# Scores of two batches joined into operations over eight array tiles, in a kernel of landmark attention, routed experts and a second layer

## The chip, the cores and the metric

One core of a Trainium2 chip runs the whole kernel. The metric is device microseconds of one execution, as the median of three runs; less is better. TensorE (PE in the profile) does the matrix products, VectorE (DVE), ScalarE (ACT) and GpSimd (POOL) the rest, and the queue of SyncE (SP) starts most of the loads.

## The reference

Three stages follow one another (4 batches, 8 heads, 576 tokens, head width 64).

```python
q_lm = q.reshape(B, H, 32, S // 32, D).mean(axis=3)      # 32 landmarks, k_lm alike
A, Bm, C = sm(q, k_lm), sm(q_lm, k_lm), sm(q_lm, k)      # sm: softmax of scaled products
Z = 2 * Z - Z @ Bm @ Z                                   # six times
x = A @ Z @ C @ v                                        # 2304 tokens x 512
h = np.maximum(x[mask] @ w1[e], 0.0)                     # e: the expert of a token, of 8
y[mask] = gate_w[mask, None] * (h @ w2[e])
r = np.maximum(y @ w_in, 0.0)                            # 512 -> 2048
out = (s * (r * r) + b) @ w_out                          # 2048 -> 512
```

`A` needs the scores of all queries with the 32 key landmarks, `C` those of the 32 query landmarks with all keys. `w_in` and `w_out` arrive as float64.

## The kernel before, in words

**A planner orders everything.** The kernel is written as a list of operations (`A(...)`, which is `Plan.add`): each has an engine or a choice of engines, a guessed duration, the buffers that it reads and writes, and a priority. `Plan.run` takes, again and again, the operation that can start first (ties by priority, then by order of writing), gives it its place in the 798 units of SBUF (256 bytes of each partition) or in the 8 banks of PSUM, and advances that engine's clock. The order of each engine that results is written into the program. So an engine works its list in order: if the chip is later at one operation than the plan had it, all behind it on that engine wait too. Where an operation may go to two engines, the planner takes the one with the earliest end, with a handicap from `TUNE["bias"]` (0.7 us against DVE, nothing against ACT or POOL): `copy` chooses between ACT and DVE, `two` and `minus` between DVE and POOL. `caps` in `Plan(...)` (L350) limits how many buffers of a name live at once.

**Attention, per batch (`attention`, L525 on).** Sums over 18 tokens make the landmarks (L558 to L565, in tile `ss`). The scores are matmuls of 64 rows by 32 columns, 288 tokens wide: `cs` (L656 to L665) for `C` and `as` (L715 to L725) for `A`. The eight heads of a batch are held as two groups `g` of four. One operation does one group: eight matmul calls, which are 16 matmul records in the trace, on four tiles of the array (two halves of the rows, each paired with two of the four strips of 32 columns), into two banks. So a batch has two `cs` and two `as` operations, each free to start when its own group is ready. After `cs` come the maximum on DVE (L671), the exponential on ACT (L679) and transposes (L687); after `as` a transpose on DVE (L730) and the softmax, whose subtraction and product are `two` operations. `TOOK` holds measured durations by name (0.75 for `cs` and `as`), and they replace the guess in the call.

**Experts.** The kernel reads which expert a batch's first token goes to, loads that expert's weights (`w1s`, `w2s`), folds the value side into the first weight (`v1`, L945) and does both layers (`experts`; all large products go through `mm3`, L972, which multiplies a high and a low part: three matmuls for one). The operation `v1` is 16 matmul records of 64 rows by 32 columns, 256 wide, on all eight tiles of the array, into two banks. The expert work of one batch runs on TensorE between the attention steps of the next ones.

**Conversion of the float64 weights (`convert`, L1037 on).** 32 loads of 512 KB (L1039) go into buffers `sg`, of which five may live at once; each takes six steps on DVE, ACT and POOL (the last is L1054) to become half of a tile `w32i` or `w32o`.

**Second layer (`layer2`, L1163 on).** Three groups G of 768 tokens, each with eight units j. A unit is seven products of 2 x 2 blocks (`prod`, each six matmuls of 384 columns), the sums of which are combined (L1198), squared on ACT and DVE (L1202, L1203), split in a high and a low part (`gh` L1206 on ACT, `rr` L1208 on DVE), and eight products with `w_out` (sums in L1250). Group 0 also prepares the parts of the weights (`weights`, `outer`, by `copy` and `minus`, L508 and L1076) and stores them; groups 1 and 2 load them back. `tokens` prepares the seven right operands of a group: loads, four sums (`tq`, L1076), then for each operand a high part `th` (a `copy`) and a low part (a `minus`). It is called for the next group in unit 7, with two gates: the first (`early`, the first product of unit 6) for the loads, the sums and the high parts of two operands, and the second (`mark`, the fifth of the seven products of unit 7) for the high parts of the five others.

Of the kernel before, what the change touches and what calls it, by code (L numbers as in the profile page):

```python
# [18 lines left out]
B, H, S, D = 4, 8, 576, 64  # L19
N, DM, E, F, DFF = B * S, H * D, 8, 1024, 2048  # L20
LM, SEG = 32, 18
NB = 288
# [296 lines left out]
TUNE = {"ahead": (6,), "t_at": lambda st: [st[B - 1]["l1half"]], "w_at": lambda st: [st[B - 1]["l1first"]], "blk": "AADD", "pre": 2, "bias": {"DVE": 0.7, "ACT": 0.0},  # L319
# [20 lines left out]
def moe_kernel(ctx, tc, qT, kT, va, vb, emb, tau, w1, w2, win, wout, s_in, b_in, outT):  # L340
    nc = tc.nc
# [8 lines left out]
    plan = Plan({"S": NS, "PS": 8}, {"sg": 5, "acc": 2, "hp": 3, "vp": 1, "w2h": 6, "w2s": 8, "v1h": 3, "v1l": 3, "w1s": 4,  # L350
# [174 lines left out]
    def attention(b, gate):  # L525
# [62 lines left out]
        def f():  # L588
            for p in range(4):
                for h in range(2):  # L590
                    nc.tensor.matmul(bs.t[row(p, h), p // 2, 0:32], ql(p)[half_(h)], kl(p)[half_(h)],
                                     start=True, stop=True)
# [65 lines left out]
        for g in range(2):  # L658
            def f(g=g):
                for hf in range(2):  # L660
                    for x in range(2):
                        for h in range(2):
                            nc.tensor.matmul(cs[g].t[row(2 * g + x, h), hf, 0:NB], ql(2 * g + x)[half_(h)],  # L663
                                             k[g][x].t[half_(h), NB * hf:NB * hf + NB], start=True, stop=True)
            A("PE", 1.07, f, r=[QS[2 * g], QS[2 * g + 1], *k[g]], w=[cs[g]], prio=pr + 3, kind="cs")  # L665
# [48 lines left out]
        am = small("am", 2, [128, 2, 2, 18])  # L714
        for g in range(2):  # L715
            aps = P("aps")
            at, tt = ats[g], S_([128, S], nm="tt")

            def f(g=g, aps=aps):
                for hf in range(2):  # L720
                    for x in range(2):
                        for h in range(2):
                            nc.tensor.matmul(aps.t[row(2 * g + x, h), hf, 0:NB], kl(2 * g + x)[half_(h)],  # L723
                                             q[g][x].t[half_(h), NB * hf:NB * hf + NB], start=True, stop=True)
            z["as"] = A("PE", 1.07, f, r=[KS[2 * g], KS[2 * g + 1], *q[g]], w=[aps], prio=pr + 4, kind="as")  # L725
# [437 lines left out]
    def layer2(G):  # L1163
# [7 lines left out]
        def unit(j, last, early):  # L1171
# [59 lines left out]
            if G + 1 < NG and j == 7:  # L1231
                tokens(G + 1, [early], [mark])
# [158 lines left out]
```

## Time and profile before

| | us |
|---|---|
| median of 3 runs (688.82 to 690.6) | 689.05 |
| the profiled execution, its own time | 693.66 |
| its span, first to last instruction | 691.8 |
| TensorE busy in the span | 648.0 |
| VectorE busy | 470.5 |
| ScalarE busy | 314.3 |
| GpSimd busy | 249.8 |

The profiled execution is 4.6 us longer than the median, and 1.9 us of its time lie outside of its span. A busy time is the union of an engine's instructions; a matmul's end is modelled, so starts are the surer measure of how closely matmuls follow one another. A row of busy time by stage gives the window and its length, then busy us and number of instructions of TensorE's matmuls, its weight loads, VectorE, ScalarE and GpSimd, then TensorE's granted clock as a share of 2.4 GHz, the busy share of the DMA engines and GB/s. In a list of waits a row says which instruction sat idle until which other one ended: in all, how often, and the longest.

### The profile page before, as it was taken

Reading aid. Unit: us, or ns where it says so; the run is one execution under the profiler, and the core shown is the slowest. Engines: PE = TensorE matmul, PEld = TensorE weight load, DVE = VectorE, ACT = ScalarE, POOL = GpSimd, SP = SyncE. Lnnn points to the kernel's source line nnn. Section 1 sums busy time; section 2 is a strip of 40 time slices with the busy share of each in tenths; the row PEclk is TensorE's granted clock in tenths of the full one; section 3 lists DMA queues with packets and bytes.
Section 4 is the critical chain, followed back from the end, with each engine's and each line's share of the span. In section 5 each row is a group of like instructions: output and inputs, shape, how many; then the busy total and the mean of one; then the engine's idle time right before and its main releaser. Section 6 shows DMA issues by size and latency. Waiting matters only on the chain.

```text
span 691.8 us, 13145 instructions
## 1 busy us (share of the span) xinstructions
PE 648.0 (94%) x5070; PEld 599.4 (87%) x5070; DVE 470.5 (68%) x971; ACT 314.3 (45%) x662; POOL 249.8 (36%) x213
## 2 busy tenths in 40 slices
PE   8789899999889998989989989999999999999995
PEld 5557778878779998978888989999999899999995
DVE  6775686688679667889899788635546744465552
ACT  2256426726445644565454464534333544333431
POOL 3641535634444574695755775000003600000000
PEclk9899999999999999999999999999999999999999
DMA  6617586575364655254747557875448476564202
GB/s 217 227 41 262 188 254 229 189 268 174 117 213 139 237 181 184 100 228 180 260 176 238 197 212 247 287 242 206 145 167 285 154 267 236 186 197 168 92 0 97
DMA packets 55577, 132.99 MB, mean 192 GB/s; under 512 B 5024, under 2 KB 25032, under 8 KB 55504
## 3 DMA queue, kind: packets, MB, share of 16 engines
q1 hardware_dynamic: 46208, 101.74, 43.7%
q10 hardware_dynamic: 9296, 30.30, 11.2%
q8 instruction: 42, 0.69, 0.4%
q14 instruction: 31, 0.25, 0.1%
HBM read 98.19 MB, written 33.84 MB: 191 GB/s over the span
## 4 chain that ended last, share of the span: by engine, by line
PE 70%; DVE 16%; ACT 5%; issue 3%; DMA 3%; POOL 1%; SPq 0%; ACTq 0%; DVEq 0%; POOLq 0%
PE big L972 60%; DVE rr L1203 3%; DVE rr L1208 2%; DMA w1s<-in_w 2%; PE big L723 1%; PE big L436 1%; PE big L825 1%; PE big L663 1%; PE big L644 1%; DVE sums L1250 1%; ACT rr L1202 1%; PE big L945 1%; DVE tq L1076 1%; DVE sg L1042 1%; DVE xx L1198 1%
## 5 line engine op out<-in xcount | busy, mean ns | idle before, releaser
L972 PE MATMUL big<-gh,rp 128*128 128x384 f32 x256 | 85.9, 335 | 1.1 <-DVE sums L1250 1.1
L972 PE MATMUL big<-rr,rp 128*128 128x384 f32 x256 | 85.6, 335 | 0.4 <-DVE rr L1208 0.4
L972 PE MATMUL big<-gh,rq 128*128 128x384 f32 x256 | 85.5, 334 | 0.0
L972 PE MATMUL big<-hh,w2h 128*128 128x288 f32 x256 | 79.1, 309 | 0.6 <-DVE hl L1000 0.6
L1208 DVE SCALAR_TENSOR_TENSOR rr<-rr,bbc,gh 128x384 fp32r<-128x384 f32 x96 | 68.9, 732 | 14.7 <-ACT gh L1206 14.7
L1250 DVE TENSOR_TENSOR sums<-big,sums 128x384 f32<-128x384 f32 x84 | 46.5, 553 | 46.9 <-PE big L972 46.4
L1206 ACT ACTIVATE gh<-rr,bbc 128x384 fp32r<-128x384 f32 x96 | 58.5, 616 | 43.3 <-DVE rr L1203 42.7
L972 PE MATMUL big<-hl,w2h 128*128 128x288 f32 x256 | 75.8, 296 | 0.0
L972 PE MATMUL big<-hh,w2s 128*128 128x288 f32 x256 | 75.5, 295 | 0.0
L972 PE MATMUL big<-th,rh 128*128 128x384 f32 x224 | 75.0, 335 | 0.0
L1203 DVE SCALAR_TENSOR_TENSOR rr<-xx,sbc,rr 128x384 f32<-128x384 f32 x72 | 64.2, 894 | 15.8 <-ACT rr L1202 14.6
L1198 DVE TENSOR_TENSOR xx<-big,xx 128x384 f32<-128x384 f32 x72 | 39.8, 554 | 50.4 <-PE big L972 48.2
L508 ACT COPY xx<-big 128x384 f32<-128x384 f32 x71 | 33.4, 470 | 80.5 <-PE big L972 80.2
L1202 ACT ACTIVATE rr<-xx 128x384 f32<-128x384 f32 x72 | 37.6, 523 | 43.4 <-DVE xx L1198 43.4
L972 PEld LDWEIGHTS big<-hh,w2h 128*128 128x128 f32 x256 | 48.2, 188 | 4.9 <-issue 3.1
L972 PEld LDWEIGHTS big<-gh,rp 128*128 128x128 f32 x256 | 48.0, 188 | 1.9 <-DVE sums L1250 1.7
L972 PEld LDWEIGHTS big<-rr,rp 128*128 128x128 f32 x256 | 48.1, 188 | 0.8 <-DVE rr L1208 0.8
L972 PE MATMUL big<-gh,oh 128*128 128x384 f32 x128 | 44.0, 344 | 5.0 <-DVE sums L1250 3.9
L972 PE MATMUL big<-ah,v1h 128*128 128x288 f32 x128 | 42.0, 328 | 7.0 <-DVE hl L1000 3.5
L972 PEld LDWEIGHTS big<-hh,w2s 128*128 128x128 f32 x256 | 48.4, 189 | 0.0
L972 PEld LDWEIGHTS big<-hl,w2h 128*128 128x128 f32 x256 | 48.4, 189 | 0.0
L972 PEld LDWEIGHTS big<-gh,rq 128*128 128x128 f32 x256 | 48.1, 188 | 0.0
(235 smaller groups left out, 1727.2 us busy)
## 6 DMA issues: line engine op xcount, KB each, us to landing
rh<-sw_d SPq DMA_DIRECT2D x16, 896.0 KB, 7.0
w1s<-in_w SPq DMA_DIRECT2D x16, 512.0 KB, 6.6
w2s<-in_w SPq DMA_DIRECT2D x16, 512.0 KB, 5.3
sg<-in_win SPq DMA_DIRECT2D x16, 512.0 KB, 4.4
sg<-in_wout SPq DMA_DIRECT2D x16, 512.0 KB, 4.5
rx<-sw_d SPq DMA_DIRECT2D x16, 512.0 KB, 4.1
rp<-so_d SPq DMA_DIRECT2D x16, 512.0 KB, 4.0
rq<-so_d SPq DMA_DIRECT2D x16, 512.0 KB, 4.5
```

Source lines behind the costliest of these rows:

```text
L436: nc.tensor.matmul(warm.t[:, 0:128], zero.t, zero.t, start=True, stop=True)
L508: nc.scalar.copy(out=out(), in_=in_()) if e == "ACT" else nc.vector.tensor_copy(out=out(), in_=in_())
L644: nc.tensor.matmul(xp.t[r_, 64 * g + 32 * lo:64 * g + 64], cur()[r_, g, 0, :], cur()[r_, g, lo:2, :], start=True, stop=True)
L663: nc.tensor.matmul(cs[g].t[row(2 * g + x, h), hf, 0:NB], ql(2 * g + x)[half_(h)], k[g][x].t[half_(h), NB * hf:NB * hf + NB], start=True, s ...
L723: nc.tensor.matmul(aps.t[row(2 * g + x, h), hf, 0:NB], kl(2 * g + x)[half_(h)], q[g][x].t[half_(h), NB * hf:NB * hf + NB], start=True, sto ...
L972: nc.tensor.matmul(out, w, x, start=s, stop=e, skip_group_check=more)
L1198: A("DVE", d_dve(NT), lambda: nc.vector.tensor_tensor(out=x.t, in0=pv(k)(), in1=x.t, op=ALU.add), r=[bank[k]], w=[x], prio=pu, kind="l6")
L1202: A("ACT", d_actp(NT), lambda: nc.scalar.activation(out=rr[i].t, in_=src(), func=AF.Relu), r=[b], w=[rr[i]], prio=pu, kind="rr")
L1203: A("DVE", d_dve(NT), lambda: nc.vector.scalar_tensor_tensor(out=rr[i].t, in0=src(), scalar=sbc[:, 0:1], in1=rr[i].t, op0=ALU.mult, op1=AL ...
L1206: A("ACT", d_act(NT), lambda: nc.scalar.activation(out=gh[i].t, in_=rr[i].t, func=AF.Identity, bias=bbc[:, 0:1]), r=[rr[i], (c_sb, 1)], w= ...
L1208: A("DVE", d_dve(NT), lambda: nc.vector.scalar_tensor_tensor(out=low(rr[i]), in0=rr[i].t, scalar=bbc[:, 0:1], in1=gh[i].t.bitcast(F32), op ...
L1250: nc.vector.tensor_tensor(out=sums[dc].t, in0=ac.t[:, 0:NT], in1=sums[dc].t, op=ALU.add)
```

## The change

`cs` and `as` become one function, `scores`. For batches 2 and 3 it makes one operation of both groups, with the matmul calls of the two groups in turn; its names `cs2` and `as2` have no entry in `TOOK`, so the planner takes 1.2 us for it. For batches 0 and 1 there are still two operations. DVE's handicap goes from 0.7 to 0.3 us, the cap of `sg` from five to four, and the second gate of `tokens` becomes the first.

```diff
-TUNE = {"ahead": (6,), "t_at": ..., "bias": {"DVE": 0.7, "ACT": 0.0},
+TUNE = {"ahead": (6,), "pairs": 2, "t_at": ..., "bias": {"DVE": 0.3, "ACT": 0.0},
...
-    plan = Plan({"S": NS, "PS": 8}, {"sg": 5, "acc": 2, ...
+    plan = Plan({"S": NS, "PS": 8}, {"sg": 4, "acc": 2, ...
...
-        for g in range(2):
-            def f(g=g):
-                for hf in range(2):
-                    for x in range(2):
-                        for h in range(2):
-                            nc.tensor.matmul(cs[g].t[row(2 * g + x, h), hf, 0:NB], ql(2 * g + x)[half_(h)],
-                                             k[g][x].t[half_(h), NB * hf:NB * hf + NB], start=True, stop=True)
-            A("PE", 1.07, f, r=[QS[2 * g], QS[2 * g + 1], *k[g]], w=[cs[g]], prio=pr + 3, kind="cs")
+        def scores(lm, keys, src, dst, prio, kind):
+
+            for gs in ([(0, 1)] if b >= TUNE["pairs"] else [(0,), (1,)]):
+                def f(gs=gs):
+                    for hf in range(2):
+                        for x in range(2):
+                            for h in range(2):
+                                for g in gs:
+                                    nc.tensor.matmul(dst[g].t[row(2 * g + x, h), hf, 0:NB], lm(2 * g + x)[half_(h)],
+                                                     src[g][x].t[half_(h), NB * hf:NB * hf + NB], start=True, stop=True)
+                o = A("PE", 1.2, f, r=[r for g in gs for r in (keys[2 * g], keys[2 * g + 1], *src[g])], w=[dst[g] for g in gs],
+                      prio=prio, kind=kind + "2" if len(gs) > 1 else kind)
+            return o
+        scores(ql, QS, k, cs, pr + 3, "cs")
...
+        ap2 = [P("aps") for _ in range(2)]
+        z["as"] = scores(kl, KS, q, ap2, pr + 4, "as")
...
-                tokens(G + 1, [early], [mark])
+                tokens(G + 1, [early], [early])
```

The loop over the two groups behind `as` now takes its bank pair from `ap2`; the matmuls in it are gone.

## Rows read from the trace of the kernel before

**Rows 1.** The page: span, and busy us of the engines.

```profile
span 691.8 us, 13145 instructions
...
PE 648.0 (94%) x5070; PEld 599.4 (87%) x5070; DVE 470.5 (68%) x971; ACT 314.3 (45%) x662; POOL 249.8 (36%) x213
```

**Rows 2.** Busy time by stage, columns as told under the table of times.

```profile
0.00:80.00 80.00, 65.60 (x914) 49.17 (x915) 53.87 (x174) 35.37 (x96) 37.43 (x63) 0.94 0.55 187
80.00:178.00 98.00, 97.05 (x1204) 80.28 (x1202) 72.34 (x233) 47.91 (x114) 43.91 (x37) 1.00 0.64 209
178.00:203.00 25.00, 20.24 (x180) 17.89 (x179) 18.68 (x52) 12.79 (x33) 12.08 (x7) 0.93 0.64 211
203.00:264.00 61.00, 60.67 (x476) 58.40 (x476) 45.06 (x93) 30.33 (x58) 32.35 (x23) 0.97 0.55 188
264.00:287.40 23.40, 20.77 (x145) 20.48 (x144) 18.51 (x28) 12.71 (x23) 12.09 (x8) 0.93 0.33 112
287.40:427.60 140.20, 128.17 (x697) 119.53 (x696) 121.59 (x156) 74.61 (x141) 95.26 (x70) 1.00 0.56 212
427.60:552.00 124.40, 122.81 (x703) 121.36 (x702) 73.03 (x120) 51.35 (x100) 16.68 (x8) 1.00 0.63 215
552.00:684.70 132.70, 132.66 (x765) 132.34 (x764) 66.83 (x122) 49.17 (x99) 0.00 (x0) 1.00 0.46 160
```

**Rows 3.** Waits of TensorE from 178 to 287.4 us: total, times, longest.

```profile
PE big L972 <- DVE hl L1000: 3.5, 2, 2.6
PE big L972 <- DVE rt L886: 2.8, 1, 2.8
```

**Rows 4.** Waits of TensorE in second-layer group 0, 287.4 to 427.6 us.

```profile
PE big L972 <- DVE xx L1198: 4.3, 5, 1.3
PE big L972 <- DVE sums L1250: 3.9, 5, 1.3
```

**Rows 5.** Chain that ended last, 80 to 155 us: start, length, what.

```profile
80.40 0.59 PE big L945 x16
...
91.34 1.10 PE big L723 x16
92.45 0.97 PE big L663 x16
...
96.00 1.10 PE big L723 x16
...
99.81 1.10 PE big L663 x16
...
153.72 1.10 PE big L663 x16
```

**Rows 6.** Waits of TensorE from 80 to 178 us.

```profile
PE big L972 <- DVE hl L1000: 0.6, 1, 0.6
```

**Rows 7.** The tile of the token operands: duration ns min/median/max, first and last start.

```profile
L508 ACT CAST th<-tq x9: 816/824/837, 273.6 to 545.0; 128x768 fp32r<-128x768 f32 x9
```

**Rows 8.** Waits of TensorE from 427.6 to 552 us.

```profile
PE big L972 <- DVE sums L1250: 1.1, 2, 0.7
```

**Rows 9.** VectorE by shape, group 0: count, busy us, mean ns, idle before.

```profile
L1203 DVE SCALAR_TENSOR_TENSOR rr<-xx,sbc,rr 128x384 f32<-128x384 f32 x24 | 32.4, 1361 | 6.6 <-ACT rr L1202 5.7
...
L1076 DVE TENSOR_TENSOR ol<-w32o,oh 128x512 fp32r<-128x512 f32 x1 | 1.2, 1225 | 0.0
```

**Rows 10.** VectorE by shape, group 2 (552 to 684.7 us).

```profile
L1203 DVE SCALAR_TENSOR_TENSOR rr<-xx,sbc,rr 128x384 f32<-128x384 f32 x24 | 14.7, 612 | 3.7 <-ACT rr L1202 3.6
```

**Rows 11.** GpSimd by shape, group 0.

```profile
L1076 POOL TENSOR_TENSOR ol<-w32o,oh 128x512 fp32r<-128x512 f32 x15 | 19.7, 1337 | 10.2 <-ACT oh L508 10.2
...
L1054 POOL TENSOR_TENSOR w32i<-w32i,sg 128x512 int32<-128x512 int32 x4 | 6.1, 1540 | 12.9 <-DVE w32i L1051 12.9
L1054 POOL TENSOR_TENSOR w32o<-w32o,sg 128x512 int32<-128x512 int32 x4 | 5.7, 1419 | 8.1 <-DVE w32o L1051 8.1
```

**Rows 12.** The page, loads: KB of one, us from issue to landing.

```profile
sg<-in_win SPq DMA_DIRECT2D x16, 512.0 KB, 4.4
```

More of the change, by code (lines that the diff above doesn't have):

```diff
@@ L316, in d_dma @@
     return nbytes / RATE
-TUNE = {"ahead": (6,), "t_at": lambda st: [st[B - 1]["l1half"]], "w_at": lambda st: [st[B - 1]["l1first"]], "blk": "AADD", "pre": 2, "bias": {"DVE": 0.7, "ACT": 0.0},
+TUNE = {"ahead": (6,), "pairs": 2, "t_at": lambda st: [st[B - 1]["l1half"]], "w_at": lambda st: [st[B - 1]["l1first"]], "blk": "AADD", "pre": 2, "bias": {"DVE": 0.3, "ACT": 0.0},
         "flex": {"w2l": "P", "al": "P"}, "fill": 45.0, "slack": 0.05, "duty": 0.45, "first": 12,
@@ L348, in moe_kernel @@
     dr = ctx.enter_context(tc.tile_pool(name="dr", bufs=1, space=DRAM))
-    plan = Plan({"S": NS, "PS": 8}, {"sg": 5, "acc": 2, "hp": 3, "vp": 1, "w2h": 6, "w2s": 8, "v1h": 3, "v1l": 3, "w1s": 4,
+    plan = Plan({"S": NS, "PS": 8}, {"sg": 4, "acc": 2, "hp": 3, "vp": 1, "w2h": 6, "w2s": 8, "v1h": 3, "v1l": 3, "w1s": 4,
                                      "hh": 5, "hl": 5, "acc2": 4, "accr": 1, "gh": 8, "rr": 8, "xx": 4, "hp2": 3,
@@ L714, in attention @@
         am = small("am", 2, [128, 2, 2, 18])
+        ap2 = [P("aps") for _ in range(2)]
+        z["as"] = scores(kl, KS, q, ap2, pr + 4, "as")
         for g in range(2):
[L716 to L725, printed above, removed]
+            aps, at, tt = ap2[g], ats[g], S_([128, S], nm="tt")
             th = lambda tt=tt: tt.t.rearrange("p (a b) -> p a b", b=32)
```

## The prediction

> **What bounds the kernel now.** I read the page first, for the share of each engine, then busy time by stage, then TensorE's waits in the stages where it idles, and then the chain of waits around the scores. The page shows TensorE busy for 648.0 of 691.8 us and VectorE, the next, for 470.5 [rows 1]: the kernel is a string of matmuls with 43.8 us of holes. The stages tell where the holes are, as length less TensorE's busy time [rows 2]: 14.4 us before 80, 1.0 from 80 to 178, 4.8 to 203, 0.3 to 264, 2.6 to 287.4, 12.0 in group 0 of the second layer, 1.6 in group 1, none in group 2, and 7.1 behind the last matmul. So from 80 to 178 us, where the scores of batches 2 and 3 lie, TensorE is the bound: whatever is taken off its list there, the rest moves up by. In group 0 it waits for VectorE, which is busy for 121.6 of 140.2 us.
>
> The holes after 178 us are late answers of VectorE rather than a lack of matmuls: waits for `hl` and for one copy, `rt` [rows 3], and in group 0 for `xx` and `sums` [rows 4]. An early hole costs a second time: in the windows where the granted clock stands below 1.00 (0.93 of 25 us, 0.97 of 61, 0.93 of 23.4) about 1.7 us each are lost, since TensorE runs at 1.2 in place of 2.4 GHz for a while after it has idled [rows 2].
>
> **The change, part by part. The scores.** In the chain a score operation moves TensorE on by 0.97 to 1.10 us for 16 matmul records, and there are eight for batches 2 and 3; the first four and the last are shown [rows 5]. Four `as` at 1.10 and four `cs` at 0.97, 1.10, 1.10 and 1.10 make 8.67 us, which go. In their place come four operations of 32 records. The nearest row is `v1`: also 64 rows by 32 columns, but on all eight tiles, and its 16 records take 0.59 us for 256 columns [rows 5]. With t for a turn of the tiles per column and f for what an operation costs once, `v1` is f + 2 x 256 t = 0.59 and a score operation, on four tiles, f + 4 x 288 t = 1.10; so t is 0.80 ns and f 0.18 us. Were `v1`'s eight tiles served four at a time, it would be f + 4 x 256 t, and f would come out as -3.5 us, which can't be: eight tiles do run abreast there. The joined operation has 32 records on eight tiles, four turns again: 1.10 us. Four of them are 4.40, and 4.3 us are saved. Bounds: scaling `v1` plainly gives 2 x 0.59 x 288/256 = 1.33 us each, a saving of 3.4; if the second group waits for the first, nothing is saved. I take 4.3, as `v1` has the same tiles and the same two-bank pattern.
>
> Here a page speaks against the change. The Trainium skill (TensorEngine Tiling (Array Packing), Gotcha 1: PSUM Pressure) says that tiles in different rows of the array cannot write one PSUM bank at the same time, and both row halves of each group write one bank. By that rule the joined operation would take turns and the saving would be 0; the trace disagrees, because `v1` does the same with 0.59 us.
>
> **What joining makes wait.** The joined operation needs the sums of all eight heads and four free banks of eight at once. In batch 2 the first `as` starts at 91.34 and the second at 96.00 us, and the first `cs` at 92.45 and the second at 99.81 [rows 5]; so the first group's softmax begins up to 5 to 7 us later. That is covered: expert matmuls of the batch before fill TensorE to 178 us with 1.0 us of holes [rows 2]. What isn't covered is a wait of the operation itself, since TensorE takes its list in order and every expert matmul (L972) behind it stands still. The nearest wait in this stage is 0.6 us [rows 6], the worst behind it 2.8, for a bank that a late VectorE copy gave back [rows 3]. I take one of 0.6 us; the bounds are none and 2.8 us for each of four. Sum for the scores: -4.3 + 0.6 = -3.7.
>
> **The tokens.** The second gate opens one unit sooner and more, and five copies `th` of 0.82 us on ScalarE [rows 7] with their low parts on GpSimd or VectorE go ahead into units 6 and 7. They are issued on those lists ahead of work of unit 7 (`gh`, `ol`, `rr`), which waits behind them. No load moves: these have the first gate already. What can be had is the hole at the start of the next group: 1.6 us for group 2 (all of the stage's idle time [rows 2], 1.1 of it a wait for `sums` [rows 8]). For group 1 the work moves into a stage in which VectorE is 87% busy, and I count nothing. I take half of 1.6: -0.8; bounds -1.6 and, as the same steps can hold up unit 6 instead, +1.3, the longest single wait of group 0 [rows 4].
>
> **VectorE's smaller handicap.** More copies and differences go to VectorE, fewer to ScalarE and GpSimd. In group 0 the product `rr` (L1203) takes 1361 ns on average, in group 2, where GpSimd does nothing, 612 [rows 9, 10]: 24 x 0.749 = 18.0 us of VectorE standing still, in 95.3 us of GpSimd's work, 0.19 us for one. Take the likeliest to move, `ol`: 15 on GpSimd at 1.337 us [rows 11]. All of them on VectorE would cost at most 15 x 1.225 = 18.4 us, at the price of the one that is there now [rows 9], and give back 20.1 x 0.19 = 3.8; VectorE would stand at 121.6 + 14.6 = 136.2 of 140.2 us, still not the bound but with no room. Against that, GpSimd's stalls are what makes VectorE late against its plan, and so TensorE idle. I take -1.0 of group 0's 12.0 us; bounds -6, half of them, and +4, what is left of VectorE's room turned into holes. Before 80 us, with 14.4 us of holes, the same choice is open and no row tells its sign: 0.
>
> **Four loads in flight.** A load takes 4.4 us from issue to landing [rows 12]. At 287.4 us 24 of 32 conversions are done, since eight last steps are left in group 0 [rows 11], which is enough for six of its eight units: a load that comes 4.4 us later is hidden by some 105 us (six units of 140.2/8). SP's list has the expert loads behind these, and a shorter ring holds them no longer than a load lasts. 0; if the cover were gone, +4.4.
>
> Sum: -3.7 - 0.8 - 1.0 + 0 = -5.5 us. The profiled execution would take 693.66 - 5.5 = 688.2; it is 4.6 us above the median, so the median goes from 689.05 to 683.5.
>
> **The rivals.** (A) *The forecast*, 680 to 687. For it speaks that the largest term is matmul time in a stage without holes.
>
> (B) *The groups take turns after all*, and nothing is saved on TensorE: 689.05 + 0.6 - 0.8 - 1.0 = 687.9. Against it speaks `v1`; for it, that the joined operation has twice `v1`'s records in a row, which no row shows. The rule of the Trainium skill named above stands behind it too.
>
> (C) *A wait in place of the matmuls, and slower.* The joined operation stands at the head of TensorE's list before its four banks or its last sum is there. The price of one such wait is 2.8 us [rows 3] and 1.7 for the slow clock behind it [rows 2], 4.5 in all. It decides from 6.1 us in all four (4.3 + 1.8 of gains); two of them instead of the 0.6 give 689.05 - 4.3 - 1.8 + 9.0 = 692.0. For it speaks that the whole order is made anew and the planner's guess for the new operation is a guess; against it that 80 to 178 us has only 1.0 us of holes with eight such operations now.
>
> (D) *VectorE is freed from GpSimd* in group 0, and half of its holes close: 683.5 - 5 = 678.5. For it speaks the 18.0 us that L1203 loses, against it that VectorE gets the work itself.
>
> **How the numbers follow.** About 0.3% (2.1 us) is what a measurement here can tell from no change, so faster is below 687.0 and slower above 691.1. Chances: A 0.46, B 0.17, C 0.17, D 0.20. Faster is A, D and a small part of B (0.02): 0.68; same is the rest of B, 0.15; slower is C, 0.17. The time is A's, 683.5. The range goes from 677 (D and somewhat more) to 691 (B, and the near part of C); outside of it are about 0.07 of D and 0.11 of C. Most of the chance has one sign.
>
> **What would show it.** In the profile after: two `as` and two `cs` operations of 32 records for the last two batches, at 1.0 to 1.3 us each (above 1.9 would be B); no wait of over 1 us in front of them (else C); TensorE's busy time before the second layer lower by about 4 us, and the second layer beginning that much sooner; the five `th` copies of groups 1 and 2 starting in unit 6 or early in 7; L1203 in group 0 below 1361 ns, and the holes of that stage not above 12.0 us. I am wrong if the second layer begins no sooner, or if group 0 takes longer by what the scores gave.

## The result, and the profile after

The changed kernel takes 695.43 us (median of 11 runs, 688.29 to 697.86), the kernel before 689.73 beside it (11 runs, 688.15 to 693.27): ratio 1.0062, 95% interval 1.0032 to 1.0091. It is slower by some 0.6% (0.8% between the two medians), where I had forecast 683.5 us and faster. The two profiled executions hide most of this: that of the kernel after (693.17 us) lies below its median, that of the kernel before (693.66) above its own, so their spans, 691.4 and 691.8, are nearly the same. They show where time moved; the sizes are read from medians. One more thing is on record for every execution, the mean granted clock: its median is 0.970 for the kernel after (11 executions) and 0.984 for the kernel before (22 executions beside e1 to e4). So 20.8 us of full clock are missing in a span of 693.5 us, where 11.0 are missing in one of 688.4. The difference of 9.8 us is an upper bound (an estimate) of what the lower clock costs, since TensorE's idle time loses nothing by it.

The page of the kernel after, span and busy us, beside [rows 1]:

```profile
span 691.4 us, 13169 instructions
...
PE 643.4 (93%) x5066; PEld 604.6 (87%) x5066; DVE 479.3 (69%) x1019; ACT 304.3 (44%) x634; POOL 221.6 (32%) x193
```

TensorE has 4.6 us less to do (643.4 for 648.0), VectorE 8.8 more and GpSimd 28.2 less. Busy time by stage, with the experts' end (263.9) and the starts of groups 1 and 2 (424.6 and 557.0) as limits, beside [rows 2]:

```profile
0.00:80.00 80.00, 69.17 (x958) 53.69 (x959) 57.13 (x185) 34.39 (x92) 35.97 (x64) 0.96 0.60 207
80.00:178.00 98.00, 97.24 (x1281) 83.84 (x1280) 75.43 (x266) 54.57 (x138) 36.21 (x27) 1.00 0.63 207
178.00:263.90 85.90, 84.38 (x668) 81.22 (x669) 70.24 (x132) 45.70 (x84) 49.59 (x29) 1.00 0.57 185
263.90:424.60 160.70, 136.38 (x706) 130.61 (x704) 128.90 (x187) 73.16 (x135) 85.71 (x66) 0.93 0.56 204
424.60:557.00 132.40, 129.14 (x727) 128.45 (x727) 79.14 (x127) 50.61 (x97) 14.12 (x7) 0.97 0.58 200
557.00:684.10 127.10, 127.09 (x733) 126.77 (x732) 67.94 (x124) 45.84 (x90) 0.00 (x0) 1.00 0.46 161
```

Length less TensorE's busy time is its holes. The first three stages end at 263.9 in place of 287.4: 23.5 us sooner, with 13.1 us of holes for 23.1 and 13.5 us less busy time (250.8 for 264.3). That is more than the 4.3 forecast for the scores: the granted clock is also higher there than in [rows 2]. Then group 0 takes 160.7 us for 140.2 and gives 20.5 of them back: 24.3 us of holes for 12.0, and 8.2 us more busy time (136.38 for 128.17). Nine more records are some 1.6 us of that (an estimate, at the 0.17 us between two starts); the rest goes with the granted clock, which is 0.93 of 2.4 GHz in place of 1.00. [rows 2] cuts at 552 us; up to the first matmul of group 2, at 557.6, group 1 of the kernel before takes 129.8 us. So the kernel after begins it 3.2 us sooner (424.6 for 427.8) and loses 2.6 of that again (132.4 for 129.8).

The chain of waits of the kernel after shows the joined scores (L666) beside `v1` (L944), as [rows 5] did:

```profile
94.52 0.59 PE big L944 x16
95.11 0.97 PE big L666 x32
...
100.33 1.13 PE big L666 x32
...
133.49 1.20 PE big L666 x31
...
140.54 1.13 PE big L666 x32
```

An operation with twice the records moves TensorE on by 0.97 to 1.20 us, about as one of 16 did (0.97 to 1.10). The largest wait of TensorE from 80 to 178 us is 0.6, for a transpose (`ce`), and none stands in front of a joined operation. What stands in group 0 instead, beside [rows 4]:

```profile
PE big L971 <- DVE sums L1249: 13.4, 6, 5.0
PE big L971 <- DVE xx L1197: 5.3, 4, 2.2
PE big L971 <- DVE xx L508: 3.1, 3, 1.9
```

The waits are for the same VectorE results as before, only longer (`sums` 13.4 us for 3.9). VectorE's product `rr` (L1202, L1203 in [rows 9]) fell from 1361 to 854 ns, as hoped, but VectorE has 187 instructions there for 156 and is busy for 128.90 us in place of 121.59, and GpSimd has 12 last conversion steps, not 8 [rows 11]:

```profile
L1202 DVE SCALAR_TENSOR_TENSOR rr<-xx,sbc,rr 128x384 f32<-128x384 f32 x24 | 20.3, 854 | 3.7 <-ACT rr L1201 3.0
...
L1053 POOL TENSOR_TENSOR w32i<-w32i,sg 128x512 int32<-128x512 int32 x6 | 9.2, 1526 | 16.0 <-DVE w32i L1050 11.8 <-PE big L971 4.3
L1053 POOL TENSOR_TENSOR w32o<-w32o,sg 128x512 int32<-128x512 int32 x6 | 8.1, 1358 | 23.2 <-DVE w32o L1050 23.2
```

Where inside of group 0 the lead goes is seen when both kernels are cut at the same number of matmuls. Three stretches of the kernel after, then the same three of the kernel before:

```profile
263.90:317.30 53.40, 46.00 (x245) 43.44 (x244) 45.59 (x67) 25.98 (x49) 29.62 (x24) 0.97 0.55 209
317.30:377.50 60.20, 52.60 (x272) 50.68 (x272) 50.21 (x79) 27.23 (x51) 32.22 (x28) 0.91 0.59 210
377.50:402.10 24.60, 18.27 (x91) 17.62 (x90) 18.68 (x25) 12.36 (x21) 16.47 (x12) 0.86 0.44 175
```

```profile
287.30:338.20 50.90, 44.96 (x245) 41.72 (x244) 42.79 (x56) 26.31 (x51) 33.90 (x26) 1.00 0.55 212
338.20:391.40 53.20, 49.36 (x272) 46.43 (x271) 47.63 (x66) 27.50 (x52) 34.60 (x28) 1.00 0.58 216
391.40:408.80 17.40, 16.97 (x93) 15.55 (x92) 12.98 (x17) 10.96 (x21) 12.88 (x10) 1.00 0.41 167
```

Of the lead of 23.4 us, 20.9 are left at the end of the first stretch, 13.9 at the end of the second, 6.7 at the end of the third and 3.2 at the start of group 1. So the change loses little in the first third of group 0 and most behind it. In the third stretch TensorE stands 5.0 us for one `sums`, while VectorE's list has an `sx` of 2.84 us and an `rr` of 2.15 us ahead of it. This wait of 5.0 to 5.1 us is there too in e2, e3, e5 and e6 below and not in e1, e4 and e12: it is seen only where the smaller handicap and the joined scores come together.

### The profile page after: what moved, and what is told of

Read it like the earlier page. It is cut to its first block, busy times and chain, and to the rows that moved or that the text cites. A ratio compares the mean times of both kernels' runs of the same rounds, so it can differ in the third digit from the quotient of the medians.

```text
span 691.4 us, 13169 instructions
## 1 busy us (share of the span) xinstructions
PE 643.4 (93%) x5066; PEld 604.6 (87%) x5066; DVE 479.3 (69%) x1019; ACT 304.3 (44%) x634; POOL 221.6 (32%) x193
## 4 chain that ended last, share of the span: by engine, by line
PE 76%; DVE 14%; DMA 3%; ACT 2%; issue 2%; POOL 1%; SPq 1%; DVEq 0%; ACTq 0%; POOLq 0%
PE big L971 68%; DVE rr L1207 3%; DVE rr L1202 2%; PE big L824 1%; PE big L666 1%; PE big L944 1%; DVE xx L1197 1%; DMA rq<-so_d 1%; DVE sx L1075 1%; DMA vv<-in_va 1%; PE big L644 1%; PE big L705 1%; DMA w1s<-in_w 1%; DVE sg L1041 1%; DMA sg<-in_wout 1%
## 5 line engine op out<-in xcount | busy, mean ns | idle before, releaser
L1207 DVE SCALAR_TENSOR_TENSOR rr<-rr,bbc,gh 128x384 fp32r<-128x384 f32 x96 | 70.9, 759 | 5.8 <-ACT gh L1205 5.7
L508 ACT COPY xx<-big 128x384 f32<-128x384 f32 x56 | 26.6, 476 | 92.0 <-PE big L971 83.3
L971 PE MATMUL big<-gh,oh 128*128 128x384 f32 x128 | 47.3, 370 | 16.1 <-DVE sums L1249 13.4
L1202 DVE SCALAR_TENSOR_TENSOR rr<-xx,sbc,rr 128x384 f32<-128x384 f32 x72 | 49.8, 695 | 12.6 <-ACT rr L1201 10.1
L958 POOL TENSOR_TENSOR w2s<-w2s,w2h 128x1024 fp32r<-128x1024 f32 x16 | 38.1, 2404 | 42.9 <-ACT w2h L508 31.0
```

Source lines behind the costliest of these rows:

```text
L508: nc.scalar.copy(out=out(), in_=in_()) if e == "ACT" else nc.vector.tensor_copy(out=out(), in_=in_())
L958: two(1024, lambda e, ws=ws, wh=wh: e.tensor_tensor(out=low(ws), in0=ws.t, in1=wh.t.bitcast(F32), op=ALU.subtract), "w2l", r=[wh], w=[ws], ...
L971: nc.tensor.matmul(out, w, x, start=s, stop=e, skip_group_check=more)
L1202: A("DVE", d_dve(NT), lambda: nc.vector.scalar_tensor_tensor(out=rr[i].t, in0=src(), scalar=sbc[:, 0:1], in1=rr[i].t, op0=ALU.mult, op1=AL ...
L1207: A("DVE", d_dve(NT), lambda: nc.vector.scalar_tensor_tensor(out=low(rr[i]), in0=rr[i].t, scalar=bbc[:, 0:1], in1=gh[i].t.bitcast(F32), op ...
```

## The experiments

"Experts' end" is the last expert matmul, "group 1" the first matmul of group 1, in the profiled execution; holes are TensorE's in group 0. The kernel before, run beside them, had medians of 690.38 (e1 to e4), 690.39 (e5 to e8), 690.15 (e9 to e12) and 689.83 us (e13 to e15).

| run | us | ratio, 95% | experts' end | group 0 | holes | group 1 |
|---|---|---|---|---|---|---|
| before | 689.73 | 1 | 287.3 | 140.5 | 12.0 | 427.8 |
| after | 695.43 | 1.0032 to 1.0091 | 263.9 | 160.7 | 24.3 | 424.6 |
| e1 handicap 0.7 again | 697.66 | 1.0052 to 1.0116 | 270.0 | 161.6 | 23.7 | 431.6 |
| e2 five loads again | 690.83 | 0.9969 to 1.0019 | 276.7 | 147.9 | 18.4 | 424.6 |
| e3 late gate again | 696.48 | 1.0026 to 1.0089 | 267.8 | 160.1 | 24.1 | 427.8 |
| e4 joined scores alone | 695.79 | 1.0048 to 1.0106 | 277.3 | 155.1 | 24.1 | 432.4 |
| e5 groups in turn | 692.73 | 1.0009 to 1.0052 | 264.5 | 163.4 | 24.3 | 427.9 |
| e6 no low words | 683.4 | 0.986 to 0.992 | 264.2 | 153.0 | 20.1 | 417.3 |
| e7 gate alone | 691.28 | 0.9994 to 1.0032 | 284.6 | 140.4 | 12.0 | 425.1 |
| e8 four loads alone | 698.32 | 1.0078 to 1.0133 | 275.0 | 160.5 | 25.3 | 435.5 |
| e9 joined, order kept | 701.97 | 1.0126 to 1.0210 | 293.0 | 144.6 | 14.9 | 437.5 |
| e10 joined, second layer kept | 691.21 | 0.9990 to 1.0033 | 276.4 | 149.3 | 17.7 | 425.7 |
| e11 four loads, order kept | 722.84 | 1.0432 to 1.0517 | 309.5 | 147.6 | 14.9 | 457.1 |
| e12 all but joined scores | 692.56 | 1.0018 to 1.0090 | 274.0 | 153.2 | 18.5 | 427.2 |
| e13 e10, conversions 47 later | 695.87 | 1.0059 to 1.0111 | 276.6 | 154.7 | 18.8 | 431.3 |
| e14 e10, conversions 120 later | 693.24 | 1.0027 to 1.0063 | 277.3 | 152.6 | 21.0 | 429.9 |
| e15 six loads, order kept | 697.39 | 1.0080 to 1.0145 | 286.5 | 144.3 | 16.0 | 430.7 |

### One part taken back: e1, e2, e3, e12

In the changed kernel, one line each:

```diff
-"bias": {"DVE": 0.3, "ACT": 0.0},
+"bias": {"DVE": 0.7, "ACT": 0.0},
...
-{"sg": 4, "acc": 2, ...
+{"sg": 5, "acc": 2, ...
...
-                tokens(G + 1, [early], [early])
+                tokens(G + 1, [early], [mark])
...
-"pairs": 2,
+"pairs": 4,
```

> The changed kernel with VectorE's handicap back at 0.7 us. In the changed kernel the attention and expert stage ends at 264 us (287 before) and group 0 of the second layer takes 160.6 us (140.4 before), so the question is what lengthened group 0. Theory H (the handicap put steps of the weight preparation on VectorE in front of rr and sums): group 0 falls to 145 us or less, the waits of TensorE for sums in it from 13.4 to under 6 us, and the time to 675 to 684 us. Theory R (the ring of four loads left 12 conversions in place of 8 for group 0): group 0 stays at 155 us or more, 12 conversions are left for it, 689 us or more. Theory C (group 0 cannot end before about 425 us whatever the stage before it gives): it ends at 420 to 428 us, about 690 us.

> The changed kernel with five float64 loads in flight again. Theory R: about 8 conversions are left at the start of group 0, it takes 150 us or less, and the time is 680 to 686 us. Theory H: group 0 stays at 155 us or more and its TensorE waits for sums at 10 us or more; time 690 us or more. Theory C: group 0 ends at 420 to 428 us, about 690 us.

> The changed kernel with the second gate of the tokens back at its old place in unit 7. Theory T (the early tokens crowd the end of group 0 and of group 1: holes of 5.0 us at 389 and 3.0 us at 527 us in the changed kernel): those two holes go, the half-clock windows behind them too, and the time falls by 6 to 10 us, to 685 to 689 us. Theories H and R: group 0 stays within 4 us of 160.6 and the time at 691 us or more.

> The changed kernel with the scores as two operations again (smaller handicap, four loads, early gate stay). If the parts added up, this would be the changed kernel plus the 4.3 us that the joined scores save: 699 to 700. By theory M (each edit remakes all lists, and what a list comes to is not the sum of the edits) the value is open between 690 and 702, and the joined scores' share read from this pair differs from the +5.4 us that they cost alone by more than 3 us.

The fifth load buffer (e2) wins back 4.6 us (695.43 to 690.83), which is the whole loss. Its two stages up to group 1, beside the stages of after above:

```profile
0.00:276.70 276.70, 255.70 (x2911) 221.93 (x2912) 215.72 (x590) 136.13 (x316) 125.81 (x124) 0.98 0.59 195
276.70:424.60 147.90, 129.54 (x700) 121.78 (x699) 120.42 (x176) 72.20 (x133) 80.49 (x63) 0.98 0.58 213
```

The experts end 12.8 us later than in the kernel after, and group 0 is 12.8 us shorter; group 1 starts at 424.6 in both. That is what theory C said; theory R is right on the 8 conversions left, but not on the time (680 to 686). So up to group 1 the two traces show no gain from the fifth buffer; what differs in every execution is the clock, a median of 0.980 for 0.970. And the lists of e2 are made anew too: no run gives the change five buffers in its own order, so how much of the 4.6 us is the buffer and how much another order is not shown.

The gate taken back (e3) is 1.05 us slower and the handicap (e1) 2.2 us slower, both with intervals that overlap that of the change, so neither is told from 0. Theories T and H fail: group 0 takes 160.1 and 161.6 us, and in e3 the wait of 5.0 us stays. Without the joined scores (e12) the rest takes 692.56 us, 2.9 less by the medians; but the two intervals (1.0018 to 1.0090, and 1.0032 to 1.0091 with them) lie almost on one another, so this is not told from 0 either. It is not the 699 to 700 of parts that add up, and it differs by 2.5 from the 5.4 that the scores cost alone (e4), less than the 3 that I had set as a sign.

### One part alone: e4, e7, e8

In the kernel before: e4 has the function `scores` of the change and nothing else, e7 the first gate for both, e8 four buffers (these two with the function, but two operations for every batch).

> The kernel before with the joined scores of batches 2 and 3 alone; handicap, ring and gate as before. If my term holds, TensorE's busy time is 4.3 us less than before (648.0), the joined operations take 1.1 us each, and the time is 685 to 687 us if the rest of the order is kept well. If gains ahead of group 0 are lost in it (theory C), the second layer begins 4 us or more sooner, group 0 is longer by as much, and the time is within 2 us of before.

> The kernel before with the earlier second gate of the tokens alone: the list of each engine keeps its order but for the token operands of groups 1 and 2. By my step: the idle time of group 1 (1.6 us before) is about halved, -0.8 us, so 689 to 690 us beside 690.4; the five th copies start in unit 6. By the opposite (the same conversions crowd the end of group 0, where VectorE is 87% busy): group 0 longer by 2 us or more, 692 us or more.

> The kernel before with four float64 loads in flight alone. My step took 0 for it, hidden by 105 us. Theory R (each buffer is held while its conversion waits for room or engines, so one buffer less means later conversions): 10 to 13 conversions are left when group 0 begins (8 before), group 0 takes 148 us or more (140.4 before), and the kernel 693 to 698 us. If it is hidden: 8 or 9 conversions left, 688 to 692 us.

The gate alone does nothing that can be measured. Each of the other two ends the experts sooner (277.3 and 275.0 for 287.3) and the kernel later; for e4 neither of my two cases came (685 to 687 us, or within 2 us of before). Both still lead the kernel before by 13 to 14 us when some 600 matmuls of group 0 are done, at 395 us where that one is at 408.8. The rest, up to group 1, takes that one 19.0 us (95 records). Here it is of e4 with its longest waits, then of e8:

```profile
395.10:432.40 37.30, 24.04 (x121) 22.90 (x120) 20.25 (x22) 11.02 (x20) 15.38 (x9) 0.82 0.40 151
```

```profile
PE big L971 <- ACT oh L508: 5.7, 1, 5.7
PE big L971 <- DVE ol L1075: 5.4, 1, 5.4
```

```profile
395.40:435.50 40.10, 24.42 (x120) 23.08 (x120) 23.86 (x31) 11.77 (x21) 12.62 (x8) 0.74 0.47 176
```

```profile
PE big L971 <- ACT oh L508: 9.5, 1, 9.5
```

`oh` is the high part of the last converted tile, `ol` the low part: in e8 the last two conversions end at 415 and 417 us and TensorE stands 9.5 us for what is made of them. These are not late loads: the last two were issued at 358 and 361 us, and ScalarE has done a step on both by 368, but VectorE's next steps on them stand at 411.5 in its list. e4 loses nearly as much in the same place with five buffers (18 us of its lead for 21), its last conversion ending at 413. Theory R fits e8 by its numbers (10 conversions are left at the experts' end, 8 in the kernel before; the time is 0.3 us above its range), but how much of the 7.9 us is the buffer and how much the order of lists made anew is not shown. The parts do not add: alone they cost 5.4 + 7.9 + 0.9 = 14.2 us (e4, e8, e7), the smaller handicap gives back 2.2 (e1, read in the change and not told from 0; alone it was not run), and the sum of 12.0 is more than twice the 5.1 by which the change is slower than 690.38.

### The joined operation itself: e5

The order of the lists is kept; only the calls inside of the joined operation are put otherwise, all of group 0 ahead of group 1.

```diff
-                    for hf in range(2):
-                        for x in range(2):
-                            for h in range(2):
-                                for g in gs:
+                    for g in gs:
+                        for hf in range(2):
+                            for x in range(2):
+                                for h in range(2):
```

> The changed kernel, with every engine's list in the same order, but inside the four joined score operations all matmuls of group 0 stand ahead of those of group 1. That gives back exactly what the interleaving saves. My step (eight tiles abreast, 4.3 us off a stage of TensorE without holes): the operations take 2.1 to 2.2 us each in place of 1.1, TensorE's busy time rises by 4.3 us, and the kernel takes 3 to 5 us more than the changed one (695.4), 699 us. If what is saved ahead of group 0 is lost inside it (theory C): the operations take 2.1 us too, the experts end some 4 us later than 264 us, but group 0 ends at the same time within 2 us, and the kernel stays at 694 to 697 us. If the groups take turns anyway: no difference in the operations' length.

The chain of e5:

```profile
94.89 1.17 PE big L666 x31
...
100.26 1.23 PE big L666 x32
...
133.66 1.23 PE big L666 x32
...
140.65 1.16 PE big L666 x32
```

My expectation failed: the groups run abreast also when their calls are not mixed. What saves the time is that they are neighbours on the list, on other tiles. So e5 did not put the 4.3 us back, and says nothing of where they went (its time is not told from that of the change). The Trainium skill (TensorEngine Tiling (Array Packing), Gotcha 1: PSUM Pressure) would have row tiles that write one bank take turns; neither order shows that here (0.97 to 1.23 us for 32 records).

### GpSimd's share of the conversions: e6

The changed kernel with its order kept, and GpSimd's addition, the last step of each conversion, left out: what the low words add to the second layer's weights is missing.

```diff
-        return A("POOL", d_pool(512), lambda: nc.gpsimd.tensor_tensor(out=d(), in0=d(), in1=lo(), op=ALU.add), r=[(sg, 0)],
+        return A("POOL", d_pool(512), lambda: None, r=[(sg, 0)],
```

> The changed kernel, every list in the same order, but the last step of each of the 32 conversions (the addition of the low word on GpSimd, L1053) is left out, so the low bits of the second layer's weights are missing from the output. It tells what GpSimd's part of the conversions costs: 12 of them lie in group 0, 17.3 us of its work. Theory P (GpSimd and VectorE hold each other up, so that work of the two left for group 0 lengthens it): the means of L1202 and L1207 in group 0 fall towards 612 ns, TensorE's holes in it from 24.3 to 16 us or less, and the kernel takes 6 to 14 us less, 681 to 689 us. Theory S (the conversions come late because there is no room for their tiles, GpSimd is only a bystander): group 0 stays within 4 us of 160.6 and the kernel at 692 us or more.

```profile
264.20:417.30 153.10, 133.05 (x706) 127.90 (x705) 120.12 (x187) 73.13 (x135) 67.38 (x54) 0.94 0.59 214
```

12.0 us go (695.43 to 683.4), as theory P said. GpSimd has 18.3 us less to do in group 0, and VectorE's busy time falls by 8.8 us (128.90 to 120.12) with the same 187 instructions: they had been held up. By the Trainium skill (SBUF — State Buffer, Who interferes with whom) VectorE and GpSimd share one pair of ports, which one of them holds for a whole instruction; the two sums agree with that. Two of theory P's signs fail, though. The holes are 20.1 us, not 16 or less, and the product `rr` of L1202 became longer, not shorter (854 ns in the change), while that of L1207 fell from 962 ns:

```profile
L1207 DVE SCALAR_TENSOR_TENSOR rr<-rr,bbc,gh 128x384 fp32r<-128x384 f32 x32 | 27.2, 867 | 0.9 <-ACT gh L1205 0.8
L1202 DVE SCALAR_TENSOR_TENSOR rr<-xx,sbc,rr 128x384 f32<-128x384 f32 x24 | 22.0, 929 | 3.9 <-ACT rr L1201 3.3
```

Group 0 is still 153.1 us long, so at most 7.6 of the 20.5 us are accounted for in the traces. Nor does e6 tell the ports from the step itself, without which each conversion is done sooner.

### The order kept: e9, e10, e11

These tell the edit from the remaking of all lists. Each operation of the kernel before got its place in the common order and its engine as constants, and the planner takes the first by place that can go. With FREE at 0 (e9, e11) all keep their place; with 1400 (e10) those up to about the experts' end are planned anew among themselves, on the engines that they had. e9 and e10 have the joined scores, e11 four buffers.

```diff
+        if kept:
+            for i, o in enumerate(todo):
+                o.rank, o.alts = KEPT[0][i], {KEPT[1][i]: o.alts[KEPT[1][i]]}
         while avail:
             best = None
+            if kept:
+                avail.sort(key=lambda o: o.rank)
             for o in avail:
+                if kept and best is not None and (avail[0].rank >= FREE or o.rank >= FREE):
+                    break
```

> The kernel before, with the joined scores of batches 2 and 3 as its only edit, and with the order of every engine's list, the choice of engines and the order of the loads kept as the kernel before has them; only what needs the second half's scores sooner than they now come steps back behind the joined operation (15 and 5 steps in front of the two joined 'cs', none and 2 in front of the two 'as'). Theory M (what was lost by the joined scores alone, 5.4 us, comes of the lists being made anew behind them): group 0 of the second layer keeps its 140 us (137 to 144), with 10 to 15 us of holes and at most 5 us at half clock. The stage of the batches pays for late softmax steps, which TensorE's kept list waits for: 4.3 us less matmul time, up to 6 us for each of the two batches in waits; so 686 to 698 in all, and the whole difference stands before the experts' end. Theory C (group 0 cannot end before some 424 us, since conversions and VectorE's work have to be done by then, whatever the order): group 0 becomes as much shorter or longer as the experts' end moves later or sooner than 287, and group 1 starts at 424 to 432 again.

> The kernel before with the joined scores as its only edit; the steps of the first part (up to some 99% of those before the experts' end) are put in order anew among themselves on the engines that they had, and all behind it, the second layer and most of its conversions, keeps the order, the engines and the loads of the kernel before. Theory M: the first part ends 4 to 10 us sooner than in the kernel before (277 to 283) and group 0 keeps 137 to 146 us with at most 15 us of holes, so that group 1 starts at 416 to 427 and the time is 680 to 687. Theory C: the first part ends as soon, but group 0 is longer by what was won, group 1 starts at 424 to 432 and the time is 688 to 696.

> The kernel before with four loads in flight in place of five as its only edit, the order of the lists and the choice of engines kept, except where a load finds no free buffer and steps back (7 places on the queue of loads, 6 on VectorE, 14 on ScalarE, 2 on TensorE). My prediction's reason (a load that comes later by its own 4.4 us is hidden): 690 +-2, group 0 within 137 to 144 us. Theory L (the buffers are held for long, so a load comes later by tens of us, and an engine's list then stands still before the conversion that needs it): TensorE gets new waits behind VectorE or ScalarE ahead of the experts' end or in group 0, group 0's TensorE idle time or that of the first part grows by over 5 us, and the time is 696 or more.

**e9** takes longer than either theory said (701.97 us, M's range ended at 698). As theory M has it, most of the loss lies before the experts' end (293.0 for 287.3), but 4.1 us more come in group 0 (144.6 for 140.5). Its waits from 80 to 180 us show what joining costs when nothing gives way:

```profile
PE big L717 <- ACT ce L709: 4.2, 2, 2.1
```

The first group's exponentials come late, and TensorE stands at the transposes that need them. The kernel before and then e9, up to their experts' ends:

```profile
0.00:287.30 287.30, 264.24 (x2909) 226.11 (x2910) 208.36 (x576) 139.02 (x323) 137.77 (x136) 0.96 0.57 191
```

```profile
0.00:293.00 293.00, 264.01 (x2910) 229.06 (x2911) 205.53 (x576) 140.02 (x323) 138.03 (x136) 0.94 0.56 188
```

TensorE idles 29.0 us for 23.1 and is as long busy as without the joining, at a lower granted clock: what the joined scores save is lost again by the clock. It is also no proof for a fixed end of group 0: group 1 starts at 437.5.

**e10** falls to theory C. The experts end 10.9 us sooner than in the kernel before, and group 1 starts 2.1 us sooner. The windows of the first unit of group 0, of the next two and of the rest tell where 8.8 us went; first the kernel before, then e10:

```profile
287.80:299.20 11.40, 8.26 (x44) 7.03 (x43) 9.58 (x13) 7.66 (x15) 8.75 (x8) 1.00 0.41 161
299.20:338.20 39.00, 36.21 (x198) 34.20 (x199) 32.70 (x43) 18.38 (x36) 24.65 (x19) 1.00 0.58 228
338.20:427.60 89.40, 83.31 (x455) 77.91 (x454) 78.90 (x101) 48.40 (x90) 61.46 (x44) 1.00 0.57 211
```

```profile
276.90:297.20 20.30, 11.52 (x44) 9.65 (x43) 13.44 (x21) 12.67 (x24) 11.10 (x9) 0.75 0.35 135
297.20:336.20 39.00, 36.21 (x198) 34.17 (x199) 32.16 (x43) 18.62 (x36) 26.51 (x19) 1.00 0.59 227
336.20:425.60 89.40, 83.31 (x455) 77.91 (x455) 78.99 (x101) 48.49 (x90) 61.57 (x44) 1.00 0.55 212
```

Unit for unit the rest is the same; the first takes 20.30 us for 11.40, at a clock of 0.75: 5.6 of the 8.9 us are idle, 3.3 are busy time at the lower clock. TensorE's longest wait there, and then those of the other engines from 270 to 300 us that lead to it:

```profile
PE big L995 <- DVE y L1046: 5.2, 2, 4.3
```

```profile
ACT sg L1068 <- DMA sg<-in_win: 5.3, 2, 3.4
...
DVE w32o L1072 <- ACT sg L1070: 3.0, 1, 3.0
```

TensorE needs the experts' last `y`. The matmuls for it are done, but VectorE's list has conversion steps ahead of the addition, these wait for ScalarE, and ScalarE for a load. So TensorE arrived sooner, the loads did not.

**e11** shows that wait at full size: four buffers in the same order cost 32.7 us (722.84 for 690.15); 22.2 of them are there at the experts' end. ScalarE's waits for loads from 90 us to the experts' end, in e11 and then in the kernel before:

```profile
ACT sg L1068 <- DMA sg<-in_win: 27.2, 6, 5.9
ACT sg L1068 <- DMA sg<-in_wout: 11.9, 5, 4.5
```

```profile
ACT sg L1045 <- DMA sg<-in_wout: 2.9, 3, 1.6
...
ACT sg L1045 <- DMA sg<-in_win: 1.7, 1, 1.7
```

39.1 us for 4.6, in a list on which the experts' `hh` stand behind the conversions. Theory L holds; a load is not hidden once a list has reached the step that needs it. The loads of e11 at 277.1, 281.7, 283.2, 287.1 and 296.3 us are issued just as the last step of a conversion ends (the same times to 0.1 us): they wait for a buffer. When the planner may make the lists anew (e8), ScalarE waits 7.5 us for loads, and 7.9 us are left of the 32.7.

### The seam, and a sixth buffer: e13, e14, e15

```diff
+                if o.kind in ("cv0", "cv1", "cvr", "cv2", "cvm", "cv3") and 1393 <= o.rank <= 1425:
+                    o.rank += 47
```

e13 is e10 with these lines, e14 has 120 for 47; e15 is the kernel before with its order kept and six buffers.

> The version with the joined scores and the second layer in the order of the kernel before (e10), with one more edit: the conversion steps that stand ahead of the experts' last y additions in the lists of VectorE, ScalarE and GpSimd go some 47 places of the common order further back, behind the y additions and the first token copies of group 0. Theory V (VectorE, and with it TensorE, stands behind a late load at the seam): the 4.35 us wait for y goes, the first unit of group 0 takes 11 to 14 us in place of 20.3, the later units take what they took, and the time is 682 to 687 in place of 691.2. Rival (group 0 is held by the loads and conversions that its last units need, wherever they stand): the first unit becomes shorter, but units 1 to 7 become longer by as much, group 1 starts at 424 or later, and the time stays at 689 to 693.

> The same with the same conversion steps 120 places further back in place of 47, into the second unit of group 0. Theory V: the first unit as in e13 (11 to 13 us); the conversions end somewhat later, which units 6 and 7 don't feel; 682 to 687. Rival: as in e13, and worse by what the conversions are later: 690 to 696.

> The kernel before with six loads in flight in place of five, its order kept but for 2 places on VectorE, 7 on ScalarE and 2 on TensorE, where the sixth buffer takes room that another tile had. With four in place of five the same kept order took 32.7 us more. If the buffers' number is what brings the loads late, six give back some of the 23.1 us of TensorE's idle time before the experts' end, 680 to 689; if room in SBUF is the limit, loads come no sooner, steps that found no room stand later, and it is 690 to 705.

The first three units of group 0 (the first, then the next two), to set beside those of e10; e13, then e14, with TensorE's longest wait in group 0 of e14:

```profile
277.10:294.40 17.30, 10.26 (x44) 7.97 (x43) 13.12 (x19) 9.66 (x18) 10.09 (x9) 0.86 0.39 150
294.40:341.30 46.90, 41.48 (x198) 39.51 (x199) 31.80 (x44) 21.03 (x40) 23.92 (x19) 0.83 0.51 200
```

```profile
277.80:290.20 12.40, 8.57 (x44) 6.98 (x43) 8.35 (x12) 7.07 (x15) 8.79 (x8) 1.00 0.45 180
290.20:339.90 49.70, 38.85 (x199) 36.93 (x200) 35.84 (x52) 23.32 (x45) 25.57 (x20) 0.93 0.50 193
```

```profile
PE big L997 <- DVE xx L1223: 9.8, 6, 4.5
```

e13 misses both of its cases: the first unit takes 17.30 us, not 11 to 14, the next two 7.9 us more, and its 695.87 us lie above both ranges. In e14 the first unit is down to 12.40 us, as theory V said, and the next two are 10.7 us longer (49.70 for 39.00); its 693.24 us are in the rival's range. The wait has passed from `y` to `xx`, 9.8 us over group 0 for 4.0 in e10. So V named what TensorE waited for, and the rival what it is worth: the third unit ends at 338.2, 336.2, 341.3 and 339.9 us in the kernel before, e10, e13 and e14, within 5.1 us, whichever way the steps stand. Six buffers (e15) are no cure either: 697.39 us, in the range of my second case (room in SBUF), which does not show that room is the reason; the last three loads are issued at 334 to 335 us, no sooner than the 330 to 336 of the kernel before, and group 0 has 16.0 us of holes. No version that does the whole work beats the kernel before by what can be measured; e2, e7 and e10 are not told from it.

## Why the prediction was wrong, step by step

**Four loads in flight: this step failed.** I took "a load that comes 4.4 us later is hidden by some 105 us" and wrote 0, or at the worst +4.4. Measured: +7.9 alone (e8), +4.6 in the change (e2), +32.7 with the order kept (e11). I had counted how long the weights last in group 0; what decides is that a buffer is held until its conversion has room and engines, so that fewer of them bring later loads at once for a row of conversions, and that VectorE and ScalarE work their lists in order. The experts' and group 0's own results stand behind a step that waits for its load. That much is shown with the order kept alone (e11: 39.1 us of ScalarE's waits for loads in place of 4.6). Where the lists are made anew, the cost is measured and its way is open: e8 loses its time at conversions that stand late in the lists, not at loads, and the change and e2 reach group 1 at the same time.

**The scores: right in the operation, wrong in what it is worth.** 1.10 us was forecast for a joined operation, 0.97 to 1.20 measured; rival B (turns) and the wait in front of it (rival C) did not come. "Whatever is taken off its list there, the rest moves up by" held at best to the experts' end: in e9 they end 5.7 us later, and in e10 they end 10.9 us sooner and 8.8 us are given back in group 0, of which I had myself read that TensorE waits there for VectorE. So -3.7 was the value at the end of a stage, not of the kernel. Measured at the end, the joined scores cost 5.4 us alone (e4); the 2.9 in the change (e12) are not told from 0, and nowhere do they gain.

**"That is covered."** The late softmax is covered only where the lists are made anew; kept as they were, TensorE waits 4.2 us for it and the experts end 5.7 us later (e9).

**The handicap.** -1.0 was forecast; 2.2 us less with it than without (e1), intervals overlapping: neither sign nor size is shown. `rr` did fall to 854 ns, but rival D's gain in group 0 did not come: VectorE got 31 more instructions there and was busy 7.3 us longer.

**The tokens.** -0.8 was forecast; +0.9 alone (e7) and -1.05 in the change (e3), neither told from 0.

**The clock.** I priced the slow clock behind a hole at 1.7 us, but only rival C uses it; the sum has no term for it. With the longer waits of group 0 goes a granted clock of 0.93 there for 1.00, and over all executions 0.970 for 0.984: up to 9.8 us, the estimate above.

**The side.** Rival C named the right side for a wrong reason. My own test, "I am wrong if group 0 takes longer by what the scores gave", is what happened: 23.5 us were won and 20.5 went there. What the sum left out, though rival C names it, is that any of these edits makes all lists anew, so that its terms do not add (14.2 - 2.2 for 5.1).

**What stays open.** Shown is that what the experts' end gains is lost again in group 0, and where: in e10, e13 and e14 in its first three units, where late loads and conversion steps stand ahead of what TensorE waits for and moving those steps moves the wait; in e4 and e8 in its last stretch, behind conversions that stand late in the lists; in the change itself behind its first third, where TensorE waits for later `sums` of VectorE. Not shown is which of the four coupled lists sets the end of the third unit at 336 to 341 us in the first of these, nor one cause for all three places. And the 5.7 us between the two medians don't stand in the two traces, whose spans are alike.

## What to carry to other kernels

A saving on the busiest engine is worth what is left of it at the next stage where that engine waits for another: look there before it is put into the sum. Price a buffer by how long it is held and by what stands behind the first step that waits for its load, not by the length of one transfer. Where a planner makes the order, try an edit also with the order kept, else the run measures the new order.

## What the runs showed of the hardware that was not expected

Two groups of 16 matmul records on other tiles of the array run abreast as long as they are neighbours, mixed (0.97 to 1.20 us in the kernel after, 1.24 in e9) or not (1.16 to 1.23, e5). And VectorE's instructions become shorter when GpSimd does less beside them: 8.8 us over 187 instructions for 18.3 us less of GpSimd's work (e6), that is 0.48 us for each us. Not every kind gains: the `rr` of L1202 rose by 75 ns, and what adds a matmul's result from PSUM to a tile (`xx`, `sums`) kept its 552 to 553 ns.
